# Attention values with the weights stationary, a ones column beside the values, and scores in pairs of units

## The chip, the cores and the metric

One core of a Trainium2 chip runs the whole kernel. The metric is the device time of one execution in microseconds, as a median over several runs. TensorE (PE, with its weight loads as PEld), VectorE (DVE), ScalarE (ACT), GpSimd (POOL) and SyncE (SP) each work through their own instructions in order and meet through semaphores.

## What is computed

Attention with four sink keys and a window of 128, for 4 batches of 8 heads, 768 positions and head size 64, followed by a feed-forward part that multiplies two projections:

```
scores = q k^T / sqrt(64)
keep   = key < 4  or  0 <= query - key < 128
a      = softmax(where(keep, scores, -1e9))
x      = (a v), heads side by side: 3072 x 512
out    = (((x w1) * (x w2)) w3) w_out          # 512 -> 1024 -> 1024 -> 512
```

Inputs and output are float32. On the chip the operands of PE are bf16 and its sums are fp32.

## The kernel before

**Units.** Queries are taken in blocks of 256 (t = 0, 1, 2 in a batch) and heads in pairs (r = 0 to 3, e = 0, 1 in a pair). One (batch, pair, block) is a unit; there are 48. For a block only the key blocks of 128 that the window reaches are used: `segments` (L206) lists three (two for t = 0). The four sink keys of all heads stand in one small matrix `ksbd`, whose scores `es` are made once for each block with t > 0 (L194).

**A unit's steps.** `scores` (L212): PE multiplies keys (stationary) by queries (moving) for both heads, six matmuls (four for t = 0) on 64 rows each, one head in the upper rows of the array and one in the lower; ACT takes the exponential into `ex` (L223); DVE multiplies by the 0/1 mask into `am` (L227) and, for t > 0, adds the two key blocks of each query into `cs` (L233). `values` (L238): PE holds the values of one head (128 keys by 64) stationary and moves the weights `am` past them, head 0 into the output's partitions 0 to 63 and head 1 into 64 to 127. With stationary matrices of ones it also makes each query's sum of weights, spread over 64 partitions. That is twelve matmuls for t > 0 (six of values, two with `cs`, four of sinks) and eight for t = 0. ACT turns the sums into reciprocals by a logarithm and an exponential (L266, L267), and DVE multiplies (L269), which gives x already transposed, `xT`, as the gates need it.

**The other work of PE.** `fold_w3` and `fold_mm` make w3 w_out once (L294, L305; `pw`). `gate` (L274; `pg`) makes x w1 and x w2 for a chunk of positions (256 in batch 0, else 384) and 128 columns: ACT copies the first, DVE multiplies by the second. `project` (L316; `po`) makes 128 rows of output. `transposes` (L159; `tp`) turns q and k of batches 0 and 1; those of batches 2 and 3 go by transposing DMAs on SP.

**Buffers.** PSUM has eight banks: two tiles of two banks for scores (`ps_sc`), one bank for values (`ps_av`), three for everything else (`ps_mm`). In a pool the tiles go round, so a new one waits for the oldest to be read.

**Order.** POOL issues all loads in the order of the list at L120. Everything else is a task with stages on engines (L361 to L423). A planner (L434 to L516) walks a model of the engines' times: at each step PE takes the task with the smallest wait, at equal waits the smallest priority number; scores have 4, values 3, gates 1000 and more. The generators are advanced in that order, and so each engine's instructions stand in it. A row's `started=` lists tasks that must have begun before.

Of the kernel before, what the change touches and what calls it, by code (L numbers as in the profile page):

```python
# [21 lines left out]
def kernel(  # L22
# [39 lines left out]
    ps_av = ctx.enter_context(tc.tile_pool(name="ps_av", bufs=1, space=PSUM))  # L62
    ps_mm = ctx.enter_context(tc.tile_pool(name="ps_mm", bufs=3, space=PSUM))
# [4 lines left out]
    ones = const.tile([P, 64], BF16, name="ones")  # L68
    sel = const.tile([P, H, P], BF16, name="sel")
    ones_s = const.tile([P, H, 64], BF16, name="ones_s")  # L70
# [4 lines left out]
    w3o = wp.tile([P, KFF, DM], BF16, name="w3o")  # L75
    def per_batch(name, shape, bufs):
        return [inp.tile(shape, BF16, tag=name, bufs=bufs, name=f"{name}{b}") for b in range(B)]
# [3 lines left out]
    vN = per_batch("vN", [P, NB, DM], 3)  # L81
# [5 lines left out]
    vs = per_batch("vs", [P, H, D], 2)  # L87
# [9 lines left out]
    def load_qkv(b, kb):  # L97
        for src, dst in ((k, kN[b]), (q, qN[b]), (v, vN[b])):
            nc.gpsimd.dma_start(out=heads(dst[:, kb, :]), in_=rows(src, b, kb))  # L99
# [29 lines left out]
    for x in order[1:4]:  # L129
# [9 lines left out]
    nc.vector.memset(ones[:], 1.0)  # L139
# [8 lines left out]
    os4 = ones_s[:].rearrange("p (r e) d -> p r e d", e=2)  # L148
    nc.gpsimd.affine_select(os4, os4, compare_op=ALU.is_ge, fill=0.0, base=0,
                            pattern=[[-32, NP], [-4, 2], [0, D]], channel_multiplier=1)  # L150
    nc.gpsimd.affine_select(os4, os4, compare_op=ALU.is_ge, fill=0.0, base=3,
                            pattern=[[32, NP], [4, 2], [0, D]], channel_multiplier=-1)
    for x in order[4:]:
        load(*x)
    for b in range(B):
        nc.vector.memset(ksbd[b][:], 0.0)

# [26 lines left out]
    def sink_values(b):  # L184

        vp = ps_mm.tile([P, H, D], FP32, tag="mm", name="vp")
        for h in range(H):
            nc.tensor.matmul(vp[:, h, :], sel[:, h, :], vN[b][:, 0, h * D:(h + 1) * D],
                             start=(h == 0), stop=(h == H - 1))
        yield  # L190
        nc.scalar.copy(vs[b][:], vp[:])
        yield
# [19 lines left out]
    def scores(b, r, t):  # L212
        c0 = P if t == 0 else 0
        sc = ps_sc.tile([P, 2, 512], FP32, tag="sc", name="sc")
        for i, (kb, qb, n, c) in enumerate(segments(t)):
            for e in range(2):
                hp = slice(64 * e, 64 * e + 64)
                nc.tensor.matmul(sc[:, e, c:c + n], kT[b][hp, r, kb * P:(kb + 1) * P],  # L218
                                 qT[b][hp, r, qb * P:qb * P + n],
                                 start=True, stop=True)  # L220
        yield
        ex = work.tile([P, 2, 512], BF16, tag="ex", name="ex")
        nc.scalar.activation(ex[:, :, c0:], sc[:, :, c0:], ACTF.Exp, scale=scale)  # L223
# [3 lines left out]
        nc.vector.tensor_mul(am[:, :, c0:], ex[:, :, c0:], mk)  # L227
        cs = None
        if t > 0:
# [3 lines left out]
            nc.vector.tensor_add(cs[:].rearrange("p e (a q) -> p (e a) q", q=P),  # L233
                                 a4[:, :, 0, :], a4[:, :, 1, :])
        ams[b, r, t] = am, cs
        yield

    def values(b, r, t):  # L238
        am, cs = ams.pop((b, r, t))
        av = ps_av.tile([P, 2, 256], FP32, tag="av", name="av")  # L240
        segs = [(kb, (qb - 2 * t) * P, n, c) for kb, qb, n, c in segments(t)]
        todo = []
        for kb, o, n, c in segs:
            for e in range(2):
                todo.append((e, 0, o, n, vN[b][:, kb, (2 * r + e) * D:(2 * r + e + 1) * D],
                             am[:, e, c:c + n]))
            for e in range(2):
                if t == 0:
                    todo.append((e, 1, o, n, ones[:], am[:, e, c:c + n]))
        if t > 0:  # L250
            for e in range(2):
                todo.append((e, 1, 0, 256, ones[:], cs[:, e, :]))
            sq = es[b][:, (t - 1) * 256:t * 256]
            for e in range(2):
                todo.append((e, 0, 0, 256, vs[b][:, 2 * r + e, :], sq))
            for e in range(2):
                todo.append((e, 1, 0, 256, ones_s[:, 2 * r + e, :], sq))
        first = [True, True]
        for i, (e, y, o, n, lhs, rhs) in enumerate(todo):
            nc.tensor.matmul(av[64 * e:64 * e + 64, y, o:o + n], lhs, rhs,  # L260
                             start=first[e], stop=(i >= len(todo) - 2),
                             skip_group_check=True)
            first[e] = False
        yield
        rec = work.tile([P, 256], FP32, tag="rec", name="rec")
        nc.scalar.activation(rec[:], av[:, 1, :], ACTF.Ln)  # L266
        nc.scalar.activation(rec[:], rec[:], ACTF.Exp, scale=-1.0)  # L267
        yield
        nc.vector.tensor_mul(xT[b][:, r, t * 256:(t + 1) * 256], av[:, 0, :], rec[:])  # L269
        yield  # L270
# [23 lines left out]
    def fold_w3(i):  # L294

        tp = ps_mm.tile([P, KFF, P], BF16, tag="mm", name="tp3")
        for j in range(KFF):
            nc.tensor.transpose(tp[:, j, :], w3_sb[:, i, j * P:(j + 1) * P], ident[:])
        yield
        w3t = work.tile([P, KFF, P], BF16, tag="w3t", bufs=5, name="w3t")  # L300
        nc.vector.tensor_copy(w3t[:], tp[:])  # L301
        w3T[i] = w3t
        yield
# [52 lines left out]
    def task(name, prio, gen, stages, after=(), loads=(), ring=None, started=(),  # L356
             half=False):
        tasks[name] = dict(name=name, prio=prio, gen=gen, stages=stages, after=list(after),
                           loads=list(loads), ring=ring, started=list(started), half=half)

    for i in range(KFF):  # L361
        task(("t3", i), 100 + i, fold_w3(i), [("pe", 0.5), ("dve", 0.65)], loads=[("w3", i)],
             started=[("fm", i - 5, 1)] if i > 4 else [], ring="mm")
        for n in range(2):
            task(("fm", i, n), 100.5 + i + 3 * n, fold_mm(i, n), [("pe", 0.9), ("act", 0.42)],
                 [("t3", i)], [("wo", n)], "mm")
    unit = []
    for b in range(B):
        for t in range(NT):
# [21 lines left out]
            for r in range(NP):  # L391
                after = list(qk)
                if b >= 2 and t == 0:
                    after.append(("g", b - 2, len(CHUNKS[b - 2]) - 1, KFF - 1, 1))
                task(("sc", b, r, t), 4, scores(b, r, t),
                     [("pe", 0.27), ("act", 0.83), ("dve", 0.58)] if t == 0 else
                     [("pe", 0.36), ("act", 1.05), ("dve", 1.05)], after, ring="sc",
                     started=[("sc",) + unit[-1]] + ([("av",) + unit[-3]] if len(unit) > 2 else [])
                     if unit else [])
                task(("av", b, r, t), 3, values(b, r, t),  # L400
                     [("pe", 0.42 if t == 0 else 0.68), ("act", 0.85), ("dve", 0.45)],
                     [("sc", b, r, t)] + ([("ss", b, t), ("sv", b)] if t else []),
                     [("v", b, kb) for kb in kbs], "av",
                     [("av",) + unit[-1]] if unit else [])
                unit.append((b, r, t))
    gates = []
    for b in range(B):
        for c, (t0, t1) in enumerate(CHUNKS[b]):
            last_t = (t1 - 1) // 256
            us = 0.01 + 0.65 * (t1 - t0) / 384  # L410
            for dt in range(KFF):
# [4 lines left out]
                     [("av", b, NP - 1, last_t)] + war, [("w1", n), ("w2", n)], "mm",  # L416
# [10 lines left out]
    MARGIN = {"av": 0.5}  # L427
    BACKLOG = 1.6
    free = {"pe": 0.0, "act": 0.0, "dve": 0.0, "sp": 0.0}
    rings = {n: [[0.0] for _ in range(k)] for n, k in (("mm", 3), ("sc", 2), ("av", 1))}  # L430
# [3 lines left out]
    def pe_pick():  # L434
        best = None
        for k in tasks.values():
# [9 lines left out]
            if k["ring"]:  # L446
                if rings[k["ring"]][0][0] is None:
                    continue
                est = max(est, rings[k["ring"]][0][0] + HOP)
# [18 lines left out]
    def advance(k, at):  # L468

        i = k["stage"]  # L470
        if k["ring"] and i == {"mm": 1, "sc": 1, "av": 2}[k["ring"]]:
            k["cell"][0] = at
        k["stage"] = i + 1
        if i + 1 < len(k["stages"]):
# [5 lines left out]
            queue[e].append((at + HOP, k["prio"], us, k))  # L480
# [3 lines left out]
    with tc.manual_schedule(engines={mybir.EngineType.PE, mybir.EngineType.Activation,  # L484
                                     mybir.EngineType.DVE, mybir.EngineType.SP}):
        while len(done) < len(tasks):
# [14 lines left out]
            if e == "pe":  # L501
# [3 lines left out]
                us = k["stages"][0][1]  # L505
                if k["ring"]:
# [7 lines left out]
            next(k["gen"])  # L514
            free[e] = start + us
# [35 lines left out]
```

## Time and profile before

| | us |
|---|---|
| median of 3 runs | 233.42 (232.82 to 234.14) |
| the profiled execution | 233.93 |
| its span, first to last instruction | 232.1 |
| PE busy in the span | 210.0 |
| ACT busy | 134.4 |
| DVE busy | 114.2 |
| POOL busy | 75.2 |

A row of a group of instructions gives line, engine, operation, output and inputs, count, busy time, the mean of one in ns, and the idle time before them. In the chain of waits each row is a start, a length and what the chain stood on; a PE piece lasts there until the next piece starts, so its length holds the gap behind it as well. "x12" counts matmuls. The granted clock is a share of full speed. Each matmul has a weight load (PEld) of its own.

### The profile page before, as it was taken

The page shows a single profiled execution, that of the slowest core. Times are in us where ns is not written, and L with a number is a line of the kernel's source. Part 1 is how long each engine was busy: PE and PEld are TensorE (multiplying, and loading weights), DVE is VectorE, ACT ScalarE, POOL GpSimd, SP SyncE. Part 2 cuts the span into 40 slices and gives each one's busy share as a digit, 9 for nine tenths or more (in the row PEclk, how much of TensorE's full clock was granted, in tenths as well). Part 3 has the DMA queues.
Part 4 walks back from the last instruction along what each step waited for, and adds up shares of the span by engine and source line. Part 5 has one row for each costly group of instructions (what it writes and reads, how often), then busy time and mean ns, then how long its engine had stood idle before and what let it go on. Part 6 is the DMA issues. An engine that isn't in the chain of part 4 may idle for free.

```text
span 232.1 us, 4737 instructions
## 1 busy us (share of the span) xinstructions
PE 210.0 (90%) x1888; PEld 130.0 (56%) x1888; DVE 114.2 (49%) x239; ACT 134.4 (58%) x269; POOL 75.2 (32%) x93
## 2 busy tenths in 40 slices
PE   0387389999999899999999999999999999999993
PEld 1275257687677676755555544555555456654441
DVE  7126425557867877557666633476753014340000
ACT  2024527558778988589677576877664433332432
POOL 7996653979996464830000000000000000000000
PEclk9999857999999999999999999999999999999999
DMA  4999999999999999999900022300000330001433
GB/s 66 154 174 201 164 207 184 180 155 157 158 148 161 133 157 132 136 154 155 128 3 0 0 93 91 135 3 0 3 0 4 135 137 0 4 0 63 164 138 136
DMA packets 96711, 24.44 MB, mean 105 GB/s; under 512 B 88496, under 2 KB 92592, under 8 KB 96688
## 3 DMA queue, kind: packets, MB, share of 16 engines
q0 software_dynamic: 80176, 14.69, 81.0%
q1 hardware_dynamic: 16512, 9.44, 18.8%
q8 instruction: 15, 0.25, 0.4%
q14 instruction: 8, 0.07, 0.1%
HBM read 29.36 MB, written 6.29 MB: 154 GB/s over the span
## 4 chain that ended last, share of the span: by engine, by line
PE 82%; DMA 8%; POOL 5%; ACT 2%; DVE 1%; issue 1%; POOLq 0%; ACTq 0%; DVEq 0%
PE pg L281 37%; PE po L320 18%; PE av L260 11%; PE sc L218 6%; PE pw L310 5%; DMA wo_sb<-in_moe_w_out_dram 4%; DMA w_sb<-in_moe_w_dram 4%; PE sp L198 2%; PE tp L164 2%; POOL w_sb L106 1%; ACT ex L223 1%; POOL kN_90 L99 1%; POOL qN_86 L99 1%; POOL vN_94 L99 1%; DVE w3t L301 1%
## 5 line engine op out<-in xcount | busy, mean ns | idle before, releaser
L281 PEld LDWEIGHTS <-w_sb 128*128 128x128 bf16 x576 | 53.6, 98 | 29.5 <-issue 5.4
L223 ACT ACTIVATE ex<-sc 128x1024 bf16<-128x1024 f32 (+1 forms) x48 | 44.7, 941 | 5.5 <-PE sc L218 5.5
L288 ACT COPY a_sb<-pg 128x384 f32<-128x384 f32 (+1 forms) x72 | 31.7, 442 | 26.0 <-PE pg L281 12.3
L227 DVE TENSOR_TENSOR am<-ex,maskt 128x1024 bf16<-128x1024 bf16 (+1 forms) x48 | 30.9, 644 | 14.1 <-ACT ex L223 13.3
L324 ACT COPY o_sb<-po 128x512 f32<-128x512 f32 x24 | 14.1, 586 | 26.5 <-PE po L320 26.5
L266 ACT ACTIVATE rec<-av 128x256 f32<-128x256 f32 x48 | 18.5, 386 | 12.7 <-PE av L260 11.9
L310 PE MATMUL pw<-wo_sb,w3t 128*128 128x256 bf16 x128 | 19.5, 309 | 6.1 <-DMA wo_sb<-in_moe_w_out_dram 5.0
L281 PE MATMUL pg<-xT_106,w_sb 128*128 128x256 bf16 x192 | 24.3, 273 | 0.3 <-DVE ab_110 L285 0.3
L281 PE MATMUL pg<-xT_107,w_sb 128*128 128x384 bf16 x128 | 23.2, 327 | 0.1
L281 PE MATMUL pg<-xT_108,w_sb 128*128 128x384 bf16 x128 | 22.4, 327 | 0.0
L281 PE MATMUL pg<-xT_109,w_sb 128*128 128x384 bf16 x128 | 21.0, 326 | 0.0
L267 ACT ACTIVATE rec<-rec 128x256 f32<-128x256 f32 x48 | 20.0, 416 | 1.5
L310 PEld LDWEIGHTS <-w3t 128*128 128x128 bf16 x128 | 13.0, 108 | 11.1 <-issue 5.6
L285 DVE TENSOR_TENSOR ab_113<-a_sb,pg 128x384 bf16<-128x384 f32 x16 | 8.9, 553 | 20.0 <-PE pg L281 20.0
L313 ACT CAST w3o<-pw 128x256 bf16<-128x256 f32 x16 | 5.9, 373 | 19.6 <-PE pw L310 19.2
L233 DVE TENSOR_TENSOR cs<-am 128x512 bf16<-128x512 bf16 x32 | 13.6, 425 | 1.1
L285 DVE TENSOR_TENSOR ab_112<-a_sb,pg 128x384 bf16<-128x384 f32 x16 | 8.8, 551 | 8.6 <-PE pg L281 6.1
L285 DVE TENSOR_TENSOR ab_110<-a_sb,pg 128x256 bf16<-128x256 f32 x24 | 10.0, 416 | 5.7 <-PE pg L281 4.0
L285 DVE TENSOR_TENSOR ab_111<-a_sb,pg 128x384 bf16<-128x384 f32 x16 | 8.8, 550 | 5.4 <-PE pg L281 4.7
L320 PE MATMUL po<-w3o,ab_110 128*128 128x512 bf16 x48 | 11.2, 380 | 0.0
L320 PE MATMUL po<-w3o,ab_111 128*128 128x512 bf16 x48 | 10.9, 379 | 0.0
L320 PE MATMUL po<-w3o,ab_112 128*128 128x512 bf16 x48 | 10.7, 379 | 0.0
(132 smaller groups left out, 297.2 us busy)
## 6 DMA issues: line engine op xcount, KB each, us to landing
out_dram<-o_sb SPq DMA_DIRECT2D x24, 256.0 KB, 2.0
w_sb<-in_moe_w_dram POOLq DMA_DIRECT2D x7, 512.0 KB, 9.8
wo_sb<-in_moe_w_out_dram POOLq DMA_DIRECT2D x2, 512.0 KB, 8.9
kN_90<-in_k_dram POOLq DMA_DIRECT2D x6, 128.0 KB, 10.3
qN_86<-in_q_dram POOLq DMA_DIRECT2D x6, 128.0 KB, 10.6
vN_94<-in_v_dram POOLq DMA_DIRECT2D x6, 128.0 KB, 10.0
kN_91<-in_k_dram POOLq DMA_DIRECT2D x6, 128.0 KB, 7.1
qN_87<-in_q_dram POOLq DMA_DIRECT2D x6, 128.0 KB, 6.3
```

The costliest lines, as they stand in the source:

```text
L218: nc.tensor.matmul(sc[:, e, c:c + n], kT[b][hp, r, kb * P:(kb + 1) * P], qT[b][hp, r, qb * P:qb * P + n], start=True, stop=True)
L223: nc.scalar.activation(ex[:, :, c0:], sc[:, :, c0:], ACTF.Exp, scale=scale)
L227: nc.vector.tensor_mul(am[:, :, c0:], ex[:, :, c0:], mk)
L260: nc.tensor.matmul(av[64 * e:64 * e + 64, y, o:o + n], lhs, rhs, start=first[e], stop=(i >= len(todo) - 2), skip_group_check=True)
L266: nc.scalar.activation(rec[:], av[:, 1, :], ACTF.Ln)
L267: nc.scalar.activation(rec[:], rec[:], ACTF.Exp, scale=-1.0)
L281: nc.tensor.matmul(pg[:], w_sb[:, kk, dt * P:(dt + 1) * P], xT[b][:, kk, tk], start=(kk == 0), stop=(kk == NP - 1))
L285: nc.vector.tensor_mul(ab[b][:, dt, tk], gate_a.pop((b, c, dt))[:], pg[:])
L288: nc.scalar.copy(a_sb[:], pg[:])
L310: nc.tensor.matmul(po[:], w3T[i][:, j, :], wo_sb[:, j, cols], start=(j == 0), stop=(j == KFF - 1))
L320: nc.tensor.matmul(po[:], ab[b][:, kk, m * P:(m + 1) * P], w3o[:, kk, :], start=(kk == 0), stop=(kk == KFF - 1))
L324: nc.scalar.copy(o_sb[:], po[:])
```

## The change

**Values.** In `values` the weights are now the stationary side: 128 keys by 128 queries of `am`, or of `es` for the sinks. The values move past them, 64 columns and one more of ones, so that each query's sum comes out in column 65 of its own row. `vN` is laid out with 80 columns for each head, of which the last of the 65 used is set to 1 by POOL ahead of each batch's loads; `vs` gets a 65th column from `ones_s`. A unit has ten matmuls for t > 0 (eight of 65 columns, two of 130 with both heads) and six for t = 0. `cs` and `ones` are gone. The output `av` has a query in each partition and lies in a bank of `ps_mm`, which now has four banks; `ps_av` is gone.

**Normalizing.** DVE takes a reciprocal of four columns and multiplies into `xn` (bf16). ACT's logarithm and exponential are gone.

**Transposes.** A new task `x_transposes` follows each two units: four transposes on PE into `xt`, in one bank of `ps_mm`, and one copy by ACT into `xT`. The gates wait for these instead of the values.

**Order.** The scores of an even head pair now ask for two free `sc` tiles and the odd pair's follow at priority 0; a new pair starts no sooner than 5.0 of the model's us after the last. The planner's stage times, its margin and the order in which its ACT and DVE queues are served are changed too, and `w3t` has four buffers instead of five.

The core of the diff:

```diff
-    ps_av = ctx.enter_context(tc.tile_pool(name="ps_av", bufs=1, space=PSUM))
-    ps_mm = ctx.enter_context(tc.tile_pool(name="ps_mm", bufs=3, space=PSUM))
+    ps_mm = ctx.enter_context(tc.tile_pool(name="ps_mm", bufs=4, space=PSUM))
...
-    vN = per_batch("vN", [P, NB, DM], 3)
+    vN = per_batch("vN", [P, NB, H, VS], 3)
...
-    vs = per_batch("vs", [P, H, D], 2)
+    vs = per_batch("vs", [P, H, D + 1], 4)
...
+            if i[1] == 0:
+                nc.gpsimd.memset(vN[i[0]][:, :, :, D:D + 1], 1.0)
...
+        nc.vector.tensor_copy(vs[b][:, :, D], ones_s[:])
...
-            cs = work.tile([P, 2, 256], BF16, tag="cs", bufs=4, name="cs")
-            a4 = am[:].rearrange("p e (a c q) -> p (e a) c q", c=2, q=P)
-            nc.vector.tensor_add(cs[:].rearrange("p e (a q) -> p (e a) q", q=P),
-                                 a4[:, :, 0, :], a4[:, :, 1, :])
...
-        for i, (e, y, o, n, lhs, rhs) in enumerate(todo):
-            nc.tensor.matmul(av[64 * e:64 * e + 64, y, o:o + n], lhs, rhs,
-                             start=first[e], stop=(i >= len(todo) - 2),
+        for i in range(2):
+            if t > 0:
+                q0 = (t - 1) * 256 + i * P
+                todo.append((av[:, i, :, :].rearrange("p e d -> p (e d)"), es[b][:, q0:q0 + P],
+                             vs[b][:, 2 * r:2 * r + 2, :].rearrange("p e d -> p (e d)")))
+            for kb, c in ((2 * t + i - 1, 2 * i * P), (2 * t + i, (2 * i + 1) * P)):
+                if kb >= 0:
+                    for e in range(2):
+                        todo.append((av[:, i, e, :], am[:, e, c:c + P],
+                                     vN[b][:, kb, 2 * r + e, 0:D + 1]))
+        for n, (o, lhs, rhs) in enumerate(todo):
+            nc.tensor.matmul(o, lhs, rhs, start=(n == 0), stop=(n == len(todo) - 1),
                              skip_group_check=True)
...
-        nc.scalar.activation(rec[:], av[:, 1, :], ACTF.Ln)
-        nc.scalar.activation(rec[:], rec[:], ACTF.Exp, scale=-1.0)
-        yield
-        nc.vector.tensor_mul(xT[b][:, r, t * 256:(t + 1) * 256], av[:, 0, :], rec[:])
+        rec = work.tile([P, 2, 2, 1], FP32, tag="rec", name="rec")
+        nc.vector.reciprocal(rec[:], av[:, :, :, D:D + 1])
+        xn = work.tile([P, 2, 2, D], BF16, tag="xn", bufs=4, name="xn")
+        nc.vector.tensor_mul(xn[:], av[:, :, :, 0:D], rec[:].to_broadcast([P, 2, 2, D]))
...
+    def x_transposes(b, r0, t):
+
+        xt = ps_mm.tile([P, 2, 2, P], BF16, tag="mm", name="xt")
+        for r in range(2):
+            xn = xns.pop((b, r0 + r, t))
+            for i in range(2):
+                nc.tensor.transpose(xt[:, r, i, :], xn[:, i, :, :].rearrange("p e d -> p (e d)"), ident[:])
+        yield
+        nc.scalar.copy(xT[b][:, r0:r0 + 2, t * 256:(t + 1) * 256],
+                       xt[:].rearrange("p r i m -> p r (i m)"))
...
-    MARGIN = {"av": 0.5}
+    MARGIN = {"av": 0.3}
+    URGENT = {"g": 0, "av": 0, "sc": 2}
+    PACE = 5.0
...
-            if kind == "sc":
+            if kind == "sc" and k["slots"] == 2:
                 busy = max(0.0, free["act"] - free["pe"]) + sum(q[2] for q in queue["act"])
-                est = max(est, free["pe"] + busy - BACKLOG)
+                est = max(est, free["pe"] + busy - BACKLOG, last_sc + (PACE if k["name"][1] else 0))
...
-            queue[e].append((at + HOP, k["prio"], us, k))
+            queue[e].append((at + HOP, URGENT.get(k["name"][0], 1), us, k))
```

What the planner made of it, at three places. First PE, in the first unit of batch 0's second query block, before: the values' stationary side (behind LDWEIGHTS) is `vN`, `ones`, `vs` and `ones_s`, 64 columns wide, and the output has 64 partitions.

```order
L260 MATMUL av<-am,vN_94 64x128
L260 LDWEIGHTS ones
L260 MATMUL av<-cs,ones 64x256
...
L260 LDWEIGHTS vs_118
L260 MATMUL av<-es_122,vs_118 64x256
...
L260 LDWEIGHTS ones_s
L260 MATMUL av<-es_122,ones_s 64x256
L218 LDWEIGHTS kT_102
L218 MATMUL sc<-qT_98,kT_102 128x128
```

The same unit now, `es` and `am` stationary, the scores of the next pair of units behind it:

```order
L252 LDWEIGHTS es_118
L252 MATMUL av<-vs_114,es_118 128x130
L252 LDWEIGHTS am
L252 MATMUL av<-vN_90,am 128x65
...
L221 LDWEIGHTS kT_98
L221 MATMUL sc<-qT_94,kT_98 128x128
```

The twelve matmuls on 64 partitions have become ten on 128. Second ACT, from batch 0's first query block to its second, before (`ex` the exponentials of the scores, `rec` the reciprocals, `w3o` the folded weights, `es` the sinks' weights):

```order
L223 ACTIVATE ex<-sc 128x2x384 x2
L313 CAST w3o<-pw 128x256 x2
L266 ACTIVATE rec<-av 128x256
L267 ACTIVATE rec<-rec 128x256
L223 ACTIVATE ex<-sc 128x2x384 x2
L266 ACTIVATE rec<-av 128x256
...
L313 CAST w3o<-pw 128x256
L202 ACTIVATE es_122<-sp 128x256
```

And now:

```order
L226 ACTIVATE ex<-sc 128x2x384 x2
L315 CAST w3o<-pw 128x256 x2
L226 ACTIVATE ex<-sc 128x2x384 x2
L270 COPY xT_102<-xt 128x2x256 x2
L290 COPY a_sb<-pg 128x256 x4
L315 CAST w3o<-pw 128x256
L205 ACTIVATE es_118<-sp 128x256
```

The reciprocals are gone, two copies of `xt` have come, and the copies of four gates (with the other four gates, which DVE takes, eight groups on PE) now stand ahead of the fold with the second half of `wo_sb` and of the sinks. Third DVE, in batch 0's second query block, before:

```order
L227 TENSOR_TENSOR am<-ex,maskt 128x1024
L233 TENSOR_TENSOR cs<-am 128x512
L301 COPY w3t<-tp_494 128x1024
L269 TENSOR_TENSOR xT_106<-av,rec 128x256
L301 COPY w3t<-tp_516 128x1024
```

And now:

```order
L256 RECIPROCAL rec<-av 128x4
L258 TENSOR_TENSOR xn<-av,rec 128x256
L230 TENSOR_TENSOR am<-ex,maskt 128x1024 x2
L256 RECIPROCAL rec<-av 128x4
L258 TENSOR_TENSOR xn<-av,rec 128x256
L287 TENSOR_TENSOR ab_106<-a_sb,pg 128x256 x4
```

The masks of two units follow each other, `cs` is gone, and each unit has a reciprocal and a multiply.

More of the change, by code (lines that the diff above doesn't have):

```diff
@@ L240, in values @@
-        av = ps_av.tile([P, 2, 256], FP32, tag="av", name="av")
-        segs = [(kb, (qb - 2 * t) * P, n, c) for kb, qb, n, c in segments(t)]
+        am = ams.pop((b, r, t))
+        av = ps_mm.tile([P, 2, 2, D + 1], FP32, tag="mm", name="av")
         todo = []
[L243 to L249, printed above, removed]
@@ L299, in fold_w3 @@
         yield
-        w3t = work.tile([P, KFF, P], BF16, tag="w3t", bufs=5, name="w3t")
+        w3t = work.tile([P, KFF, P], BF16, tag="w3t", bufs=4, name="w3t")
         nc.vector.tensor_copy(w3t[:], tp[:])
@@ L394 @@
                     after.append(("g", b - 2, len(CHUNKS[b - 2]) - 1, KFF - 1, 1))
[L395 to L399, printed above, removed]
+                lead = r % 2 == 0
+                task(("sc", b, r, t), 4 if lead else 0, scores(b, r, t),
+                     [("pe", 0.22), ("act", 0.83), ("dve", 0.58)] if t == 0 else
+                     [("pe", 0.28), ("act", 1.05), ("dve", 0.7)], after, ring="sc",
+                     slots=2 if lead else 1,
+                     started=([("sc",) + unit[-1]] if unit else [])
+                     + ([("av",) + unit[-3]] if lead and len(unit) > 3 else []))
                 task(("av", b, r, t), 3, values(b, r, t),
[L401 removed]
+                     [("pe", 0.2 if t == 0 else 0.37), ("dve", 0.55)],
                      [("sc", b, r, t)] + ([("ss", b, t), ("sv", b)] if t else []),
[L403 removed]
+                     [("v", b, kb) for kb in kbs], "mm",
                      [("av",) + unit[-1]] if unit else [])
                 unit.append((b, r, t))
+                if not lead:
+                    task(("xt", b, r - 1, t), 2.5, x_transposes(b, r - 1, t),
+                         [("pe", 0.24), ("act", 0.6)],
+                         [("av", b, r - 1, t), ("av", b, r, t)], [], "mm",
+                         [("xt",) + unit[-4][:1] + (unit[-4][1],) + unit[-4][2:]] if len(unit) > 3 else [])
     gates = []
@@ L470, in advance @@
         i = k["stage"]
-        if k["ring"] and i == {"mm": 1, "sc": 1, "av": 2}[k["ring"]]:
+        if k["ring"] and i == 1:
             k["cell"][0] = at
@@ L514 @@
             next(k["gen"])
+            if e == "pe" and start - free[e] > 0.3: print("model idle", k["name"], round(start,2), round(start - free[e],2))
             free[e] = start + us
```

57 lines of the change are left out of this document (25 added, 32 removed).

## The prediction

> **What bounds the kernel now.** I read the stages first, by the busy time of each engine in stretches of the span. The columns are length, busy us and instructions of PE, PEld, DVE, ACT and POOL, then granted clock, DMA share and GB/s.
>
> ```profile
> 0.00:32.10 32.10, 15.57 (x152) 12.50 (x153) 14.52 (x29) 9.25 (x18) 25.45 (x36) 0.93 1.48 157
> 38.00:60.00 22.00, 21.34 (x274) 16.49 (x272) 13.97 (x29) 15.13 (x32) 18.46 (x23) 1.00 2.26 163
> 60.00:100.00 40.00, 39.19 (x467) 28.62 (x465) 28.49 (x67) 31.51 (x71) 27.87 (x33) 1.00 2.13 146
> 100.00:140.00 40.00, 39.58 (x364) 21.89 (x363) 24.42 (x52) 30.72 (x60) 1.03 (x2) 1.00 0.70 75
> 140.00:188.70 48.70, 48.70 (x387) 25.77 (x386) 22.52 (x47) 30.42 (x59) 0.00 (x0) 1.00 0.13 49
> ```
>
> Up to 32.1 us PE is busy for half the time. From 38 us it is idle for 0.66 + 0.81 + 0.42 = 1.9 us up to 140 us and then never, while ACT and DVE have slack in every stretch. So after the loading stage a microsecond of PE's stream is a microsecond of the end. The chain of waits gives that stream, piece by piece (start, us, what):
>
> ```profile
> 21.91 10.19 DMA wo_sb<-in_moe_w_out_dram
> 32.15 1.86 PE pw L310 x8
> 34.01 0.85 PE sp L198 x4
> 34.86 0.97 PE sc L218 x12
> 35.83 1.82 PE pw L310 x8
> 37.65 0.50 PE tp_494 L298 x8
> 50.43 0.45 PE tp L164 x8
> 52.71 0.48 PE sp L198 x4
> 53.19 0.55 PE sc L218 x12
> 53.73 0.98 PE pw L310 x8
> 62.05 0.44 PE pg L281 x4
> 74.07 0.23 PE vp L188 x8
> 99.25 0.44 PE sc L218 x8
> 101.33 0.27 PE sc L218 x4
> 102.35 0.45 PE av L260 x8
> 164.04 0.67 PE av L260 x12
> 164.70 0.33 PE sc L218 x6
> 165.03 2.71 PE pg L281 x16
> 188.68 20.80 PE pg L281 x128
> ```
>
> Three things are in it. From 164.04 to 167.74 us stands one steady period: values 0.67, scores 0.33, sixteen gate matmuls 2.71. The tail from 188.68 us is gates and projections alone. And the gates there take 20.80/128 = 0.1625 us each, so sixteen would be 2.60; behind a unit they are 0.11 longer. Values address the array in two column halves and scores in two row halves; gates and projections use all of it. I read the 0.11 as the price of changing between these shapes. A change of output tile is not its cause: the 128 gates change tile every four matmuls at no price.
>
> In the loading stage, PE, DVE and POOL (rows of the timeline; in brackets how long the engine was idle before, and what ended it):
>
> ```profile
> 24.32 0.30 PE L260 MATMUL av<-am,vN_94 128*64 128x256 bf16 x2 [0.95 <-DVE xT_106 L269]
> 26.45 0.30 PE L260 MATMUL av<-am,vN_94 128*64 128x256 bf16 x2 [1.60 <-DVE xT_106 L269]
> 28.35 0.42 PE L260 MATMUL av<-am,vN_94 128*64 128x256 bf16 x2 [1.38 <-DVE xT_106 L269]
> 24.55 1.26 DVE L227 TENSOR_TENSOR am<-ex,maskt 128x768 bf16<-128x768 bf16 x2 [0.28 <-ACT ex L223]
> 24.86 0.70 POOL L106 DMA_DIRECT2D w_sb<-in_moe_w_dram  x1 [2.08 <-DMA w_sb<-in_moe_w_dram]
> ```
>
> The one av bank makes each unit's values wait for the unit before to pass ACT and DVE; the fourth comes at 28.35 though its scores were masked at 25.8. Then the second half of wo_sb holds PE to 32.15. The clock falls in this hole:
>
> ```profile
> 26.00:28.00 2.00, 0.52 (x8) 0.38 (x8) 0.53 (x2) 0.80 (x2) 1.47 (x3) 0.85 2.31 160
> 28.00:30.00 2.00, 1.65 (x17) 1.48 (x17) 0.29 (x1) 0.74 (x2) 2.00 (x3) 0.50 1.61 194
> 36.00:38.00 2.00, 2.00 (x16) 1.51 (x14) 1.47 (x3) 1.38 (x2) 0.63 (x1) 0.59 1.31 201
> ```
>
> It is 0.50 at 28 us and is full again only near 37.5 us, about 5.3 us after PE took up continuous work at 32.15.
>
> **The change part by part.** *Values.* A unit past the first query block had twelve matmuls (0.67). Now it has eight of 65 moving columns and two of 130, all 128x128 stationary. The trace has that form: vp, 128x128 stationary and 64 columns, takes 0.23/8 = 0.029 us each; the transposes (128 columns) take 0.45/8 = 0.056. So 8 x 0.029 + 2 x 0.056 = 0.345. A first-block unit falls from 0.45 to 6 x 0.029 = 0.175. No row shows an output that starts at an odd column; the bounds are 0.029 below and 0.056 above, and I take vp's, the same shape but for one column.
>
> *Against it* speaks the time of a weight load. The groups:
>
> ```profile
> L281 PEld LDWEIGHTS <-w_sb 128*128 128x128 bf16 x576 | 53.6, 98 | 29.5 <-issue 5.4
> L266 ACT ACTIVATE rec<-av 128x256 f32<-128x256 f32 x48 | 18.5, 386 | 12.7 <-PE av L260 11.9
> L267 ACT ACTIVATE rec<-rec 128x256 f32<-128x256 f32 x48 | 20.0, 416 | 1.5
> L324 ACT COPY o_sb<-po 128x512 f32<-128x512 f32 x24 | 14.1, 586 | 26.5 <-PE po L320 26.5
> L233 DVE TENSOR_TENSOR cs<-am 128x512 bf16<-128x512 bf16 x32 | 13.6, 425 | 1.1
> L269 DVE TENSOR_TENSOR xT_108<-av,rec 128x256 bf16<-128x256 f32 x12 | 5.0, 421 | 7.1 <-ACT rec L267 7.1
> L181 DVE COPY ksbd_117<-kT_105 64x16 bf16<-64x16 bf16 x2 | 0.3, 162 | 0.0
> ```
>
> A load of 128 columns lasts 98 ns. But vp's eight loads and matmuls go by at 29 ns a pair, so the loads overlap one another there, and I cost them at nothing; if they did not, see the first rival. The Trainium skill's page "TensorE: Matmul & The Clock Gate" (Back-to-back issue gap) gives about 81 ns for each matmul of a sustained load-and-matmul stream with 128 columns; by that the 416 value matmuls and 96 transposes would be 41.5 us, 22 more than in my sum. The rows disagree with it: 56 ns for transposes and 29 for vp.
>
> *Transposes* are new: four for each pair of units, 4 x 0.056 = 0.225, on PE's path.
>
> *Scores in pairs.* Two adjacent units take 0.55 where two alone take 0.66, and there is one change of shape behind them, not two. For first blocks the pair is 0.44.
>
> A pair past the first block: before 2 x (0.67 + 0.33 + 0.11) = 2.22; now 2 x 0.345 + 0.225 + 0.55 + 0.11 = 1.575; saved 0.645, sixteen times: 10.3. A first-block pair: 2 x (0.45 + 0.27 + 0.11) = 1.66 against 0.35 + 0.225 + 0.44 + 0.11 = 1.125; saved 0.535, for the six of batches 1 to 3: 3.2. Batch 0's first block lies in the loading stage and is counted below. By the order three counted pairs had adjacent scores already (0.22 each): -0.7. Sum 12.8.
>
> *Loading stage.* ACT's two steps per unit and the single bank go; the fourth unit's am is there at 25.8 at the latest. Then values 0.3, reciprocal and multiply 0.6, transposes about 0.3, copy 0.6: xT is complete near 27.3, where eight gate groups now stand ahead of the transposes and pw. Their weights are there: at 24.86 POOL saw a load of w_sb land, and by its order (w3, w1, w2) I take that for w2's first half, the last that they need. At the low clock four 256-column matmuls take 1.86/2 = 0.93, else 0.44. If the clock needs 5.3 us of work again, 5.7 groups go slowly and 2.3 fast: done at 33.6; two transposes 0.9; pw at 34.5 instead of 32.15: +2.35. In return 8 x 0.44 = 3.5 us of gates are off the later stream, and the pieces from 32.15 to 38.15 (6.0 us at low clock) take 0.98 + 0.48 + 0.55 + 0.98 + 0.45 = 3.44: -2.56. The skill's same page (Part 1: The HAM clock gate) puts the warm-up at a window of about 3.4 us; by that pw comes at 33.5, a microsecond better; the 5.3 us here are longer, so I keep them.
>
> *DVE* loses cs (13.6) and 48 multiplies of 0.42, and gets 48 reciprocals and 48 multiplies. The reciprocal of four values per partition isn't shown: at least the smallest copy's 0.16, at most the 256-wide 0.42; I take 0.16, since width sets those rows. Net -6 us, at the upper bound +7. *ACT* loses 18.5 + 20.0 and gets 24 copies of 128x512 at 0.586: -24 us. Neither is on PE's path, so both count nothing as long as the four shared banks come free in time. Queued behind a late bank are the gates on PE.
>
> *POOL and queues.* Four memsets of 48 values per partition stand ahead of each batch's loads; the two ones_s selects shrink. The DMA engines work without pause there, and the loads keep their sizes. The last memset waits for batch 0's values, as v's loads of batch 3 did: nothing. The tiny ones copies on DVE hide behind w3's landing.
>
> Sum: -12.8 + 2.35 - 3.5 - 2.56 = -16.5 us. The profiled execution took 233.93 us (span 232.1), so 217.4; the three runs have a median 0.5 lower, and I say 217.0.
>
> **The rivals.**
>
> *Weight loads bound (slower).* If consecutive stationary operands of computed data did not overlap, each of 416 + 96 would take the row's 98 ns: 50.2 us against the 19.2 in my sum (32 x 0.345 + 16 x 0.175 + 24 x 0.225), +31, so 248. It turns the sign once the mean matmul costs 16.5/512 = 32 ns more than I have. For it: PEld's duration. Against it: vp and the transposes, at this clock and with the same loads. By the page's 81 ns it is 239.
>
> *New waits.* The values now release a bank only after reciprocal and multiply, the transposes need both units' products, and all share one ring with the gates. If PE stands 0.4 us for each of 22 pairs, 9 us come back: 226. For it: DVE and ACT are busy for 71 and 79 per cent of 60 to 100 us, and less time remains for their work. Against it: both lose work, and the order puts gates between a pair's values and its transposes.
>
> *The early hole stays.* If xT of the first block comes later than wo_sb, nothing fills the hole: -12.8 alone, 220.6.
>
> *Half the price of the values.* If 65 columns at odd offsets cost what 128 do, 416 x 0.027 = 11 us come back: 228. The same size results if the 0.11 us gaps belong to something other than the array's shape and stay: some 90 of them, 10 us, 227.
>
> **How the numbers follow.** Forecast 0.72 (213 to 221: the clock's return, the old 1.9 us of idle, a few us of new waits); new waits 0.12; the hole 0.08; half price or gaps that stay 0.04; weight loads 0.04. The range 213 to 226 holds the forecast, the hole and most of the new waits. Half a per cent (1.2 us) is about what a measurement of this kernel can tell from no change. Faster 0.95, same 0.01, slower 0.04.
>
> **What would show it.** In the new profile: values of ten matmuls in about 0.35 us of the chain and of six in 0.18; transposes of four in 0.225; gates behind values without the extra 0.11; the first gates near 27 us; PE idle about 2 us between 38 and 140 us; the final stretch of gates and projections unchanged in length, begun 16 us earlier. The forecast is wrong if value matmuls start more than 40 ns apart, if PE waits on xn, xt or a shared bank for over 5 us, or if the first gates come after 32 us.

## The result, and the profile after

The changed kernel takes 226.55 us (median of 4 runs, 224.78 to 227.49) where the kernel before takes 233.42 (4 runs, 232.82 to 234.14): a ratio of 0.970, 95% interval 0.962 to 0.977. It is faster, by 6.9 us and not by the 16.5 of the forecast, and it lies half a microsecond outside the range. The profiled execution took 225.83 us, its span 224.0.

The stages first, in the same columns as before (length, busy us and instructions of PE, PEld, DVE, ACT and POOL, granted clock, DMA share, GB/s):

```profile
0.00:32.10 32.10, 19.44 (x161) 14.27 (x162) 13.94 (x36) 8.52 (x15) 24.59 (x37) 0.89 1.48 161
32.10:38.00 5.90, 5.84 (x71) 4.91 (x69) 2.90 (x6) 3.28 (x8) 2.27 (x3) 1.00 1.31 200
38.00:60.00 22.00, 22.00 (x304) 19.77 (x302) 14.05 (x31) 13.47 (x28) 17.77 (x23) 1.00 2.29 162
60.00:100.00 40.00, 37.99 (x488) 28.98 (x485) 29.43 (x77) 27.77 (x52) 25.16 (x30) 1.00 1.85 133
100.00:140.00 40.00, 33.55 (x309) 20.55 (x312) 21.00 (x50) 21.18 (x34) 5.44 (x7) 0.87 0.87 96
```

Up to 100 us it is as forecast: the clock is full from 32 us on, and PE has hardly a gap. From 100 to 140 us PE stands for 6.45 us and its clock is 0.87, where before it stood for 0.42 at full clock. In pieces of 4 us, from 98 us:

```profile
98.00:102.00 4.00, 1.69 (x16) 0.86 (x13) 0.00 (x0) 1.10 (x3) 4.00 (x6) 1.00 2.23 148
102.00:106.00 4.00, 0.00 (x0) 0.00 (x0) 0.93 (x4) 0.00 (x0) 3.44 (x4) 0.54 2.02 132
106.00:110.00 4.00, 3.66 (x26) 2.02 (x27) 2.29 (x6) 1.76 (x3) 0.00 (x0) 0.50 1.88 155
110.00:114.00 4.00, 4.00 (x21) 2.34 (x20) 2.31 (x4) 1.84 (x4) 0.00 (x0) 0.68 1.68 156
114.00:118.00 4.00, 4.00 (x54) 2.94 (x53) 2.89 (x8) 2.78 (x5) 0.00 (x0) 1.00 1.36 182
```

DVE, ACT and PE all stop between 97.8 and 99.7 us while the DMA engines go on. PE's clock is half when it resumes, and full only in the last row: 3.66 x 0.50 + 4.00 x 0.32 = 3.1 us are lost to it. With the stall of 6.65 us itself that is 9.8 us, and without them the profiled execution would have taken 225.83 - 9.8 = 216.0 us, a microsecond under the forecast's 217.0. So the whole miss stands at one place. The chain of waits through it (start, us, what):

```profile
98.21 0.18 PE av L252 x6
98.39 0.27 PE pg L283 x2
98.66 6.31 DMA kT_101<-kN_89
...
104.99 0.44 DVE ksbd_113 L184
...
105.64 0.19 DVE rec L256
...
105.86 0.44 DVE xn L258
...
106.34 1.46 PE pg L283 x4
```

The chain goes over to a DMA, the one that transposes batch 3's first keys (`kT_101`). Behind it stands a 64x16 copy of batch 3's sink keys on DVE (`sink_keys`, L184), behind that in DVE's queue the reciprocal and multiply of a unit of batch 2, and for that unit's bank in `ps_mm` waits a gate. The waits of PE and of POOL name the two ends (us in total, times, longest):

```profile
PE pg L283 <- DVE xn L258: 6.7, 1, 6.7
```

```profile
POOL kN_89 L100 <- DMA qT_96<-qN_84: 10.2, 1, 10.2
```

POOL waited 10.2 us before it could issue the first load of batch 3's keys, and the timeline gives the time (with DVE's last work before the copy):

```profile
93.21 0.87 POOL L100 DMA_DIRECT2D kN_89<-in_k_dram  x1 [10.23 <-DMA qT_96<-qN_84]
...
97.27 0.55 DVE L230 TENSOR_TENSOR am<-ex,maskt 128x768 bf16<-128x768 bf16 x1
...
98.66 2.84 SPq L176 DMA_TRANSPOSE kT_101<-kN_89  x2
104.99 0.62 DVE L184 COPY ksbd_113<-kT_101 64x16 bf16<-64x16 bf16 x2 [7.18 <-DMA kT_101<-kN_89]
```

In the kernel before, POOL's timeline has that load 13.3 us earlier:

```profile
79.88 0.88 POOL L99 DMA_DIRECT2D kN_93<-in_k_dram  x1
```

The reason stands in the waits of POOL's instructions. `qN` and `kN` have two buffers for four batches. By these waits batch 3's keys now lie in batch 2's buffer, which batch 2's transposing DMAs must have read first; before, no instruction of POOL waited for such a DMA, so they lay in the other one. No line of the diff says this; the first experiment tests it. Yet the same copy of the sink keys, in the trace of before (count, duration in ns, first and last start):

```profile
L181 DVE COPY ksbd_117<-kT_105 x2: 157/162/168, 108.2 to 108.4; 64x16 bf16<-64x16 bf16 x2
```

came at 108.2 us, 3.2 us later than now, and nobody waited for it. So the late load by itself may be no loss. What changed is that PE and DVE now come to this point at 98 us, and the data do not.

### The profile page after: what moved, and what is told of

It reads as the page before. It is cut to its first block, busy times and chain, and to the rows that moved or that the text cites. A ratio compares the mean times of both kernels' runs of the same rounds, so it can differ in the third digit from the quotient of the medians.

```text
span 224.0 us, 4640 instructions
## 1 busy us (share of the span) xinstructions
PE 199.1 (89%) x1882; PEld 133.8 (60%) x1888; DVE 109.2 (49%) x258; ACT 110.4 (49%) x197; POOL 75.2 (34%) x97
## 4 chain that ended last, share of the span: by engine, by line
PE 69%; DMA 18%; POOL 7%; DVE 3%; issue 1%; SPq 1%; ACT 1%; POOLq 0%; ACTq 0%; DVEq 0%
PE pg L283 31%; PE po L322 18%; PE pw L312 6%; DMA kN_88<-in_k_dram 5%; PE av L252 4%; PE sc L221 4%; DMA qN_84<-in_q_dram 3%; DMA w_sb<-in_moe_w_dram 3%; DMA qT_96<-qN_84 3%; DMA kT_101<-kN_89 3%; PE xt L268 2%; PE sp L201 1%; PE tp L167 1%; POOL vN_92 L100 1%; POOL vN_90 L100 1%
## 5 line engine op out<-in xcount | busy, mean ns | idle before, releaser
L283 PEld LDWEIGHTS <-w_sb 128*128 128x128 bf16 x576 | 54.7, 100 | 33.8 <-DVE xn L258 7.0
L226 ACT ACTIVATE ex<-sc 128x1024 bf16<-128x1024 f32 (+1 forms) x48 | 44.1, 954 | 13.2 <-PE sc L221 12.7
L230 DVE TENSOR_TENSOR am<-ex,maskt 128x1024 bf16<-128x1024 bf16 (+1 forms) x48 | 30.3, 644 | 13.6 <-ACT ex L226 13.0
L283 PE MATMUL pg<-xT_103,w_sb 128*128 128x384 bf16 x128 | 26.7, 347 | 6.7 <-DVE xn L258 6.7
L283 PE MATMUL pg<-xT_102,w_sb 128*128 128x256 bf16 x192 | 25.7, 281 | 0.3 <-ACT xT_102 L270 0.2
L283 PE MATMUL pg<-xT_104,w_sb 128*128 128x384 bf16 x128 | 22.6, 326 | 0.0
L258 DVE TENSOR_TENSOR xn<-av,rec 128x256 bf16<-128x256 f32 x48 | 20.4, 425 | 1.7
L283 PE MATMUL pg<-xT_105,w_sb 128*128 128x384 bf16 x128 | 21.0, 326 | 0.0
L252 PEld LDWEIGHTS <-am 128*128 128x128 bf16 x352 | 17.1, 98 | 3.2 <-DVE am L230 0.8
L312 PEld LDWEIGHTS <-w3t 128*128 128x128 bf16 x128 | 13.3, 109 | 7.9 <-issue 2.9
L256 DVE RECIPROCAL rec<-av 128x4 f32<-128x4 f32 x48 | 8.6, 178 | 12.8 <-PE av L252 12.5
L322 PE MATMUL po<-w3o,ab_106 128*128 128x512 bf16 x46 | 11.1, 379 | 0.1
L268 PE MATMUL xt<-ident,xn 128*128 128x128 bf16 x96 | 10.1, 226 | 1.2 <-DVE xn L258 0.8
L322 PE MATMUL po<-w3o,ab_108 128*128 128x512 bf16 x47 | 10.6, 379 | 0.1
```

What stands on the lines that cost most here:

```text
L252: nc.tensor.matmul(o, lhs, rhs, start=(n == 0), stop=(n == len(todo) - 1), skip_group_check=True)
L258: nc.vector.tensor_mul(xn[:], av[:, :, :, 0:D], rec[:].to_broadcast([P, 2, 2, D]))
L268: nc.tensor.transpose(xt[:, r, i, :], xn[:, i, :, :].rearrange("p e d -> p (e d)"), ident[:])
L283: nc.tensor.matmul(pg[:], w_sb[:, kk, dt * P:(dt + 1) * P], xT[b][:, kk, tk], start=(kk == 0), stop=(kk == NP - 1))
L312: nc.tensor.matmul(po[:], w3T[i][:, j, :], wo_sb[:, j, cols], start=(j == 0), stop=(j == KFF - 1))
L322: nc.tensor.matmul(po[:], ab[b][:, kk, m * P:(m + 1) * P], w3o[:, kk, :], start=(kk == 0), stop=(kk == KFF - 1))
```

## The experiments

Each was run beside the kernel before on its chip.

| kernel | median us (range) | ratio to before (95% interval) |
|---|---|---|
| after | 226.55 (224.78 to 227.49) | 0.970 (0.962 to 0.977) |
| e1_own_slots | 224.41 (224.18 to 224.7) | 0.960 (0.956 to 0.964) |
| e2_sink_later | 226.5 (225.42 to 227.51) | 0.969 (0.964 to 0.973) |
| e3_before_shared | 233.15 (232.59 to 234.26) | 0.999 (0.996 to 1.001) |
| e4_in_order | 222.55 (220.38 to 223.29) | 0.950 (0.945 to 0.956) |
| e5_shared_in_order | 226.34 (224.49 to 226.8) | 0.967 (0.962 to 0.972) |
| e8_told_late | 217.26 (215.84 to 218.7) | 0.931 (0.925 to 0.938) |
| e11_told_again (the same kernel) | 218.01 (216.44 to 219.27) | 0.936 (0.931 to 0.941) |
| e9_in_order_told | 218.09 (217.29 to 219.1) | 0.935 (0.930 to 0.940) |
| e7_gates_later | 224.74 (222.06 to 224.85) | 0.960 (0.953 to 0.967) |

### Batch 3's loads in batch 1's buffers

```diff
-    def per_batch(name, shape, bufs):
-        return [inp.tile(shape, BF16, tag=name, bufs=bufs, name=f"{name}{b}") for b in range(B)]
+    def per_batch(name, shape, bufs, slots=None):
+        return [inp.tile(shape, BF16, tag=f"{name}s{slots[b]}" if slots else name,
+                         bufs=1 if slots else bufs, name=f"{name}{b}") for b in range(B)]
...
-    qN = per_batch("qN", [P, NB, DM], 2)
-    kN = per_batch("kN", [P, NB, DM], 2)
+    qN = per_batch("qN", [P, NB, DM], 2, (0, 1, 0, 1))
+    kN = per_batch("kN", [P, NB, DM], 2, (0, 1, 0, 1))
```

> Batch 3's k and q get batch 1's buffers instead of batch 2's; POOL then issues all six v loads of batch 3 ahead of its first k load. PE, ACT, DVE and SP keep the order of the changed kernel. Theory A (batch 3's first keys land too late, and the copy of sink keys that waits for them blocks DVE's queue): the 10.2 us wait of POOL for batch 2's transposes goes, but six v loads stand first at about 0.85 us each, so k lands some 2 us earlier than at 98.5; the PE stall shrinks from 6.7 to 4 or 5 us: 223 to 225. Rival B (late data leave PE without work, whatever DVE's order): 223 to 225 as well. Rival C (the stall is not what costs the time; ten-matmul values and the new waits do): 226.5, no change.

224.41 us: 2.1 us better than the changed kernel, though the intervals of the two ratios overlap. POOL's 10 us wait is gone, but the stall is not:

```profile
PE pg L283 <- DVE xn L258: 5.1, 1, 5.1
```

The build had also set the order of POOL's loads anew. All six blocks of batch 3's values now go ahead of its first keys, which are issued at 87.25 us instead of 93.21. So the buffer is only one of the things that hold these loads.

### The sink keys' copy planned later

```diff
-                task(("sk", b), 0, sink_keys(b), [("dve", 0.2)], [qk0[0]])
+                task(("sk", b), 0, sink_keys(b), [("dve", 0.2)],
+                     [qk0[0]] + ([("av", 2, 3, 1)] if b == 3 else []))
```

> The loads stay as in the changed kernel; batch 3's copy of sink keys comes later in DVE's order, behind the values of batch 2's second query block. Theory A: DVE no longer waits in front of work that is ready, kT of batch 3 still lands near 105 us, the 6.7 us stall of PE and about 3 us of low clock behind it go: 216 to 219. Rival B: batch 3 is needed when it is late, so PE stands elsewhere for the same time: 225 to 227. Rival C: 226.5.

226.5 us, no change. DVE's copy no longer holds anything, and PE stands at another place, the sinks' scores, which wait for batch 3's transposed queries (PE's waits, then the window):

```profile
PE sp L201 <- DMA qT<-qN: 8.4, 3, 6.5
```

```profile
110.00:120.00 10.00, 2.85 (x35) 1.65 (x32) 2.60 (x7) 3.26 (x5) 0.00 (x0) 0.81 1.54 141
```

PE is busy for 2.85 of 10 us. DVE's queue was only where the wait showed first; that it is the cause by itself has fallen. The stall is that of PE's fixed order, which goes on to batch 3 before batch 3's data are there.

### The kernel before, with batch 3's loads held up

```diff
+    qN = per_batch("qN", [P, NB, DM], 2, (0, 1, 0, 0))
+    kN = per_batch("kN", [P, NB, DM], 2, (0, 1, 0, 0))
```

> The kernel before, with batch 3's k and q in batch 2's buffers, so that POOL waits there for batch 2's transposes and issues four v loads first, as in the changed kernel. Theory B: the kernel before reaches batch 3 about 10 us later, its copy of sink keys at 108 us, so late loads cost it little: 233 to 235. If the shared buffers alone made the stall: 240 to 243.

233.15 us, a ratio of 0.999 (0.996 to 1.001). Its POOL waits as long as that of the changed kernel,

```profile
POOL kN L99 <- DMA kT<-kN: 10.6, 1, 10.6
```

its first keys of batch 3 are issued at 92.10 us, and it loses nothing. The late loads alone cost nothing; they cost the changed kernel its 9.8 us because it arrives some 10 us sooner.

### POOL's loads in written order, with own and with shared buffers

```diff
-    for x in order[4:]:
-        load(*x)
+    with tc.manual_schedule(engines={mybir.EngineType.Pool}): [load(*x) for x in order[4:]]
```

e4 has this and the buffers of e1, e5 has this alone.

> Batch 3's k and q in batch 1's buffers, and POOL's loads in the written order k, q, v by key block. PE, ACT, DVE and SP keep the changed kernel's order. Theory A: the first k of batch 3 lands near 88 us and its transpose near 96, before DVE reaches the copy at 97.8; stall and low clock go: 215.5 to 218.5. Rival B: the same. Rival C: 225 or more.

> POOL's loads in the written order, but batch 3's k and q in batch 2's buffers as in the changed kernel. Theory A: POOL still stands before the first k until batch 2's last transpose lands at 93, and now v of batch 3 stands behind it too, so PE waits for v's first block near 96 us as well: no gain, 226 to 230. If the order of the loads alone were the cause: 217. Rival C: 226.5.

e4 takes 222.55 us, 4.0 better than the changed kernel; e5 takes 226.34. PE's waits in e4:

```profile
PE vp L191 <- DMA vN<-in_v_dram: 2.7, 1, 2.7
PE sp L201 <- DMA qT<-qN: 1.7, 1, 1.7
```

and in e5:

```profile
PE vp L191 <- DMA vN<-in_v_dram: 6.6, 1, 6.6
PE sp L201 <- DMA qT<-qN: 2.3, 1, 2.3
```

With own buffers the keys come in time and the values, which in that order stand behind them, are late by 2.7 us. With shared buffers POOL stands again, and the values behind the keys wait with them. The order of the loads changes which of them PE meets and for how long (4.4 us of these waits in e4, 8.9 in e5), but in none of these orders do all of batch 3's data come in time for the faster stream.

### The planner told that batch 3 comes later

```diff
                         task(qk[-1], 1, transposes_dma(src, dst, kb),
-                             [("sp", 1.4), ("dma", 6.5)],
+                             [("sp", 1.4), ("dma", 6.5 if b == 2 else 16.5)],
```

No load and no buffer differs in the source; the planner alone believes that batch 3's transposes land 10 us later, and so orders PE's work otherwise. e9 is e4 with the planner told 8 us more, for the transposes (14.5) and for batch 3's values.

> The changed kernel with its loads and buffers as they are; only the planner is told that the transposes of batch 3's k and q land 10 us later, so it puts gates and projections ahead of what needs them, on all engines. Theory B (the shorter values bring PE to batch 3's data before the loads do, and its fixed order makes it stand there, at whichever instruction comes first): all the late instructions move behind work that is ready, the stall and the low clock go: 216 to 218.5. If lateness itself cost the time (not enough ready work): 224 to 227. Theory A with DVE's queue alone: as the run with the copy moved, 226.5.

> Batch 3's k and q in batch 1's buffers, loads in written order, and the planner told that batch 3's v lands 8 us later and its transposes 8 us later. Theory B: PE waits for nothing of batch 3; 215.5 to 218, four to six under the run with the loads in order alone (222.55). If its remaining waits had been harmless: 222.

> The paired kernel whose planner is told that batch 3's transposes land 10 us later, as the yardstick on the same chip: 217.3 by both theories, between 215.8 and 218.7.

217.26 us, and 218.01 in six more runs: the time of the forecast, and 9 us under the changed kernel. POOL still waits 10.3 us, the keys are still issued at 92.14. The stages of e8:

```profile
60.00:100.00 40.00, 38.50 (x496) 29.43 (x495) 31.33 (x82) 27.86 (x52) 25.52 (x31) 1.00 1.91 139
100.00:140.00 40.00, 39.01 (x393) 23.81 (x388) 22.88 (x55) 26.41 (x44) 4.47 (x6) 1.00 0.95 113
```

PE stands for 1.50 + 0.99 = 2.5 us from 60 to 140 us (and for none from 38 to 60), at full clock throughout: the "about 2 us" of the prediction. PE does gates of batch 1 and units of batch 2 while batch 3 lands. Counted by the columns that the matmuls have moved (half for a matmul on half the array, and 384 columns in 0.1625 us as in the last 128 gates), the changed kernel is 0.3 us of full-clock work behind e8 at 80 us and 9.3 us behind at 140, so what e8 gains it gains here.

With better loads as well, e9 (218.09) is no faster. As expected, PE waits for nothing of batch 3 there, but it stands for batch 2's queries, in front of the sinks' scores of its last block at 94.46 us:

```profile
PE sp L201 <- DMA qT<-qN: 3.1, 1, 3.1
```

The loads in that order thus bring a wait of their own, and whether an order made for them would gain more was not tested.

### The early gates left out of the loading stage

```diff
-                     [("xt", b, NP - 2, last_t)] + war, [("w1", n), ("w2", n)], "mm",
+                     [("xt", b, NP - 2, last_t)] + war
+                     + ([("fm", 0, 1)] if (b, c) == (0, 0) else []), [("w1", n), ("w2", n)], "mm",
```

on top of e8: the gates of batch 0's first block may not run before the fold with the second half of `wo_sb`.

> The same base (217.26), with batch 0's first gates planned only after the first fold with the second half of wo_sb, as before the change. My term: the eight groups no longer fill the wait for wo_sb (+3.5 us) and PE meets the folds at the low clock (+2.6), while the folds start some 2 us earlier (-2.4): 3.7 us slower, 220 to 222. If the loads bound the stage anyway: 217.

224.74 us, 7.5 over e8 where 3.7 were expected. The profile has the expected part, a clock of 0.67 from 32 to 38 us, and a second one (stages of e7):

```profile
32.10:38.00 5.90, 5.90 (x58) 4.23 (x57) 1.43 (x3) 3.44 (x6) 1.88 (x3) 0.67 1.31 199
60.00:100.00 40.00, 35.53 (x436) 27.40 (x435) 26.92 (x70) 24.95 (x47) 28.91 (x35) 0.92 2.06 142
```

```profile
PE sp L201 <- DMA qT<-qN: 2.9, 1, 2.9
```

PE is busy for 3.0 us less than in e8 from 60 to 100 us, and its clock falls to 0.92 of those 40 us. It is the same trouble with another batch: the sinks' scores of batch 2's last query block wait for its queries until 94.6 us (in e8 they stand at 92.65 and wait for no DMA). The two parts can be told apart by the columns that the matmuls have moved, counted as above: PE in e7 is 3.3 us of full-clock work behind e8 at 38 us, still 3.3 to 3.4 at 60 and at 80, and 8.7 at 100. So the early gates are worth about what was forecast, in one profile of each, and the rest is the second stall.

### Scores one unit at a time

e8 with the scores of every unit as a task of its own: 42 blocks of scores on PE in place of 24.

```diff
-                task(("sc", b, r, t), 4 if lead else 0, scores(b, r, t),
+                task(("sc", b, r, t), 4, scores(b, r, t),
...
-                      slots=2 if lead else 1,
+                      slots=1,
...
-            if kind == "sc" and k["slots"] == 2:
+            if kind == "sc":
...
```

> The changed kernel with the planner told of batch 3's late transposes (217.26), and scores planned one unit at a time as before the change. By its order PE has 42 separate blocks of scores instead of 24. My term of the prediction (0.11 us lost at each change between half-array scores and full-array work, two for each block): 18 blocks x 0.2 = 3.6 us slower, 220 to 222. If the adjacency were worth nothing: 217. The order of the gates among the units moves too, which may cost or gain a microsecond.

> Scores one unit at a time, once more and with more runs, beside the same kernel with pairs. If the pairs are worth what the prediction gave them (22 pairs by about 0.22 us, 18 more blocks of scores each with its own change of shape), this is about 4 us slower than the paired one: 221 to 222. If they are worth nothing because the single kernel has room elsewhere, both come within 1 us, 217 to 218.

The four runs of e6 took 218.14, 222.21, 222.74 and 222.8 us, the six of e10 218.39, 218.94, 220.17, 222.87, 223.13 and 223.76. They fall into two groups, four runs from 218.14 to 220.17 us and six from 222.21 to 223.76, at about the same granted clock (0.98 to 0.99), so the table has no row for them. The lower group is 1 to 3 us above the median of e8, less than the 4 of the prediction's term; the upper is 5 to 6.5 above it. What parts the groups was not shown. Within the lower one, the profiled run of e10 (220.17 us) has a wait which that of e6 (218.14) hardly has:

```profile
PE vp L191 <- DMA vN<-in_v_dram: 2.4, 1, 2.4
```

This order is again one that meets its loads at the moment of their landing. What the pairs are worth by themselves stays open: about 1 us by the middle of the lower group, and no run settles it.

## Why the prediction was right, and where it failed

**The step that failed** is the one under "POOL and queues": "The DMA engines work without pause there, and the loads keep their sizes. The last memset waits for batch 0's values, as v's loads of batch 3 did: nothing." With it fell "PE idle about 2 us between 38 and 140 us". Two things were missed. The rotation of buffers was taken as it was, though the build set it anew; the order of POOL's instructions, with four loads of batch 3's values now ahead of its first keys, could have raised the question. And the sentence before it held the reason for the cost: if the DMA engines have no pause, batch 3's data cannot come much earlier, while the sum brought PE to them 10 us earlier. In e4 the first load of batch 3's keys goes out at 75.27 us, 4.6 earlier than before, and still SP's first transpose of them starts at 90.09, only 2.2 earlier. DVE had finished the work in front of the sink keys' copy at 97.8 us, and before it came to that copy at 108.2: some 10 us of the sum were earned ahead of the meeting point, and most of that came back there. The experiments together show it: late loads cost the slow kernel nothing (e3); better loads alone return 2 to 4 us (e1, e4); another order of the engines' work returns all of it (e8).

**The terms of the sum** hold as pieces of the chain. From the chain of waits after, in batch 3:

```profile
150.35 0.22 PE xt L268 x4
150.57 2.60 PE pg L283 x16
153.17 0.71 PE av L252 x20
153.89 0.55 PE sc L221 x12
154.44 1.41 PE pg L283 x8
156.71 0.36 PE av L252 x10
157.07 1.30 PE pg L283 x8
```

Ten value matmuls take 0.36 us (forecast 0.345, before 0.67), four transposes 0.22 (0.225), the pair's scores 0.55 (0.55). Behind values and transposes sixteen gates take 2.60 and eight 1.30, without the extra 0.11; behind scores eight take 1.41, with it. A pair is 0.71 + 0.22 + 0.55 + 0.11 = 1.59 where 1.575 was forecast. That answers the slower rival (weight loads) and that of half the price: both are out. The forecast's objection to the 81 ns in the Trainium skill's page "TensorE: Matmul & The Clock Gate" (Back-to-back issue gap) stands as well: 0.71/20 = 36 ns with changes from 65 to 130 columns included.

**The loading stage**, in the chain after:

```profile
28.78 4.34 PE pg L283 x30
...
34.94 0.60 PE sp L201 x4
35.54 0.55 PE sc L221 x12
36.08 1.85 PE pw L312 x16
```

PE's timeline has the first two gate matmuls at 27.91 us and the other thirty from 28.78, 0.6 and 1.5 later than forecast; they are done at 33.1 (forecast 33.6), since the clock was back sooner (0.84 from 30 to 32 us). The first fold with the second half of `wo_sb` starts at 33.84, where 34.5 was forecast and 32.15 was before: +1.7 for the term of +2.35. The chain passes this fold by, since it goes over DVE's copies of the transposes; the `pw` that it shows at 36.08 are the next folds. The clock is full from 32 us on, as the term of 2.56 had it. The rival of the hole that stays did not come about.

**DVE and ACT.** Reciprocals and multiplies, by group:

```profile
L258 DVE TENSOR_TENSOR xn<-av,rec 128x256 bf16<-128x256 f32 x48 | 20.4, 425 | 1.7
L256 DVE RECIPROCAL rec<-av 128x4 f32<-128x4 f32 x48 | 8.6, 178 | 12.8 <-PE av L252 12.5
L268 PE MATMUL xt<-ident,xn 128*128 128x128 bf16 x96 | 10.1, 226 | 1.2 <-DVE xn L258 0.8
```

The reciprocal takes 178 ns, near the lower bound of 0.16 that was taken. ACT is busy for 110.4 us where it was 134.4, the forecast's -24; DVE for 109.2 where it was 114.2, against a forecast of -6.

**The rival of new waits** named 226, which is nearly what came, but not for its reason. It spoke of 0.4 us at each of 22 pairs; PE's waits on `xn` in transposes are 0.8 us in all, and the one long wait on `xn` is the tail of a DMA. A right number from a wrong rival tells nothing. The sign that the prediction named, a wait on `xn` of over 5 us, did appear, and following it to the DMA gave the cause.

**The final stretch** keeps its length, and its beginning measures the whole stream. The last 128 gates begin at 188.68 us before, and in the changed kernel at 180.65 us, in e8 (its chain of waits) at 171.31:

```profile
171.31 20.80 PE pg L283 x128
```

That is 8.0 and 17.4 us sooner, where 16 were forecast.

## What to carry to other kernels

When the engine that sets the pace gets faster, ask for each transfer whether its end moves too: every fixed queue now meets its data earlier, and a gain in front of a landing that stays is given back there, with a clock that has to come up again on top. Compare the waits of the loading engine's instructions in the two builds, since buffers that go round can be dealt out otherwise though no line on them changed. And a planner's landing times have to be set again when the work in front of them shrinks: one number there was worth 9 us, while better loads without it were worth 2 to 4.

## What the runs showed of the hardware

The clock's return differs: full about 6.2 us after PE resumed at 106.34 us in the changed kernel (0.50 from 106 to 112, 0.86 from 112 to 114), and about 5.5 after 32.15 in the kernel before (0.50 from 32 to 36, 0.59 from 36 to 38; the forecast read 5.3). In the Trainium skill, "TensorE: Matmul & The Clock Gate" (Part 1: The HAM clock gate) gives a free-running window of about 3.4 us; both returns are longer than one window and shorter than two, and these runs show no more of it than that. In the loading stage the clock fell to 0.50 in the profile after (28 to 30 us) and not at all in that of e8, with PE busy for 1.75 and 1.41 of those 2 us; in the profile after it was back sooner, full from 31 us, about 2 us after the gates began to run without a gap at 28.78.

Stationary operands computed only just before are no dearer: the loads of `am` last 98 ns each, and their matmuls of 65 columns, with outputs that start at odd columns, go by at the pace of `vp`'s 64: six in 0.18 us, 0.030 each, against 0.029.

Runs of one kernel spread by 2 to 3 us: 2.9 over the four of e8 (215.84 to 218.7), 2.8 over the six of e11, and 2.6 over the 13 of the kernel before that ran beside e8. The landing of a load is a likely source (2.4 us of wait in e10's profile, 0.4 in that of e6, which was 2.0 us faster); that it is the only one was not shown.
